# Holding back one batch's V load in a fused attention + MLP kernel: V of batch 3 behind the last x transpose of batch 2

## The chip, the cores and the metric

One core of a Trainium2 chip runs the whole program. The metric is device time in microseconds (us). The profile shows one execution with its own zero, so its span is some 2 us below the time. "Before" is the kernel as it was, "after" the changed one.

## The reference, cut to what matters

```python
# q, k, v: [8 batches, 8 heads, 576, 64]; w_in [512, 2048]; w_out [2048, 512]
scores = q @ k^T / 8 + alibi bias, masked to a causal window of 128
attn   = softmax(scores)
x      = (attn @ v) as [8*576 tokens, 512]
h      = x @ w_in
out    = (h * cos(h)) @ w_out
```

Tokens of all batches are one long row for the MLP, which runs in 9 chunks of 512 tokens. A batch has 576 tokens, so a chunk needs x of two batches: chunk 2 (tokens 1024 to 1535) begins in batch 1 and needs the first blocks of batch 2 almost at once.

## The kernel before

A planner in the kernel takes all operations with their dependences and estimated durations, orders them for each engine, and emits them with semaphores. It models the DMA engines too, so a changed dependence of a load can reorder TensorE's work far away from it. GpSimd issues all loads, in program order; the sync queue (SP) issues the transposes and the stores.

```python
def load_v(b, order=range(NBLK), after=()):
    for t in order:
        rows = 128 if t < 4 else 64
        op("pool", [lambda e, t=t, rows=rows: e.dma_start(
            vp[b % 2][0:rows, t, :, 0:64],
            v[b, :, 128 * t:128 * t + rows, :].rearrange("h p d -> p h d"))],
           r=[("vinit", b % 2)], w=[("v", b % 2, t)], dma=f"ldv{b % 2}{t}", ..., after=after)
...
def x_back(b, u, s, i):            # one head pair, 256 tokens of x: to xT (features x tokens)
    ...
    pr, G = u
    t0 = S * b + 256 * G
    if (b, pr + 4 * G) not in XPE:     # batches 0 and 1 do it on TensorE, the others by DMA
        o = op("sp", [lambda e: e.dma_start_transpose(
            xT[:, pr, t0:t0 + 256].rearrange("p (r t) -> p r t", r=2), xnat[i][:, :])],
            r=[("xnat", i)], w=xkeys(pr, t0, 256), dma=f"xb{i}", ...)
        xops.append(o)
        return
    ...
# main loop; moe1 is x @ w_in (L855 half chunks, L840 whole), moe2 is @ w_out (L866)
for c in range(NCH):
    ...                                # moe1 of chunk c
    second = moe2(c)
    if c + 1 < B:
        ...                            # attention of batch c + 1: scores, exp, mask, PV, x_back
    if c == 0:
        load_qk(2)
        load_v(2)
        load_qk(3)
        load_v(3)
    else:
        if 3 < c + 2 < B:
            load_v(c + 2, after=xops[3:4] if c > 2 else xops[-1:])
        if c + 3 < B:
            load_qk(c + 3, xops[-1:])
    ...                                # moe2 of chunk c, filled in around the attention
```

`xops` holds the nine x transposes of the batch in hand: head pairs 0 to 3 for the first 256 tokens, pairs 4 to 7 (the same heads, next 256 tokens), then the tail of 64 tokens. V has two buffers, so V of batch 3 goes where V of batch 1 was.

The softmax here doesn't subtract the row's maximum and nothing guards it: scores larger than these inputs give would overflow.

## Time and profile before

| | before |
|---|---|
| time, median of 3 | 313.44 us (313.19 to 313.70) |
| span of the profiled execution | 311.0 us |
| TensorE busy | 302.8 us, 97% |
| waits of TensorE for DMA after 21 us | one, 1.29 us, at the start of chunk 2 |
| first scores of batch 2 to those of batch 3 | 31.68 us |
| first scores of batch 3 to those of batch 4 | 30.34 us |

Three habits of reading serve here. First, ask TensorE's waits: on an engine that is full, the few gaps are all that a change outside it can win. Second, compare stages by a mark that recurs once a batch (the first scores, `L634 x12` in the chain of waits), and count the matmuls between the marks. Third, for a DMA read the time from issue to landing (its "flight" below), not the size: here it depends on what else is queued. A line of a timeline reads: start in us, length in us, engine, line of the kernel, operation, output<-inputs, shapes, count, and in brackets the idle time before it and what ended that. A line of a DMA queue gives packets, MB, and the time that its packets took as a share of the 16 engines' time, which can pass 100% where packets overlap. "Pair" is a head pair of x; "PV" is the product attn @ v. The prediction shows the lines of the kernel before.

### The profile page before, as it was taken

Reading aid. Unit: us, or ns where it says so; the run is one execution under the profiler, and the core shown is the slowest. Engines: PE = TensorE matmul, PEld = TensorE weight load, DVE = VectorE, ACT = ScalarE, POOL = GpSimd, SP = SyncE. Lnnn points to the kernel's source line nnn. Section 1 sums busy time; section 2 is a strip of 40 time slices with the busy share of each in tenths; the row PEclk is TensorE's granted clock in tenths of the full one; section 3 lists DMA queues with packets and bytes.
Section 4 is the critical chain, followed back from the end, with each engine's and each line's share of the span. In section 5 each row is a group of like instructions: output and inputs, shape, how many; then the busy total and the mean of one; then the engine's idle time right before and its main releaser. Section 6 shows DMA issues by size and latency. Waiting matters only on the chain.

```text
span 311.0 us, 6735 instructions
## 1 busy us (share of the span) xinstructions
PE 302.8 (97%) x2676; PEld 177.0 (57%) x2676; DVE 196.2 (63%) x443; ACT 205.8 (66%) x300; POOL 105.7 (34%) x134
## 2 busy tenths in 40 slices
PE   7799999999989999999999999999999999999996
PEld 4478546884578558845844454455445444444444
DVE  3898666786678748874885568767874881353000
ACT  7798946886478659765885478748874984462211
POOL 8999868620007300970555046405000000000000
PEclk9999999999999999999999999999999999999999
DMA  8999999999949992999999999999823100101112
GB/s 131 170 194 192 192 171 193 157 140 173 192 70 127 153 145 70 142 146 196 113 168 174 152 169 111 150 159 138 146 64 103 36 0 34 71 0 67 70 67 101
DMA packets 160894, 39.24 MB, mean 126 GB/s; under 512 B 148960, under 2 KB 156384, under 8 KB 160864
## 3 DMA queue, kind: packets, MB, share of 16 engines
q0 software_dynamic: 109552, 18.10, 78.7%
q1 hardware_dynamic: 51312, 20.72, 36.3%
q8 instruction: 21, 0.34, 0.5%
q14 instruction: 9, 0.07, 0.1%
HBM read 36.70 MB, written 9.44 MB: 148 GB/s over the span
## 4 chain that ended last, share of the span: by engine, by line
PE 91%; DMA 4%; DVE 2%; POOL 2%; issue 0%; ACT 0%; POOLq 0%
PE ps L866 39%; PE ps L855 20%; PE ps L840 20%; PE ps L634 4%; PE ps L728 3%; DMA knat<-in_k_dram 2%; DMA xT<-xnat 2%; PE ps L731 2%; PE ps L547 1%; PE ps L714 1%; PE ps L716 1%; DVE p L689 1%; PE ps L624 1%; POOL vp L464 1%; PE ps L803 1%; DVE emtail L528 0%
## 5 line engine op out<-in xcount | busy, mean ns | idle before, releaser
L866 PE MATMUL ps<-w_outb,gT 128*128 128x512 bf16 (+2 forms) x592 | 137.9, 374 | 0.0
L832 DVE TENSOR_TENSOR gT<-ps,cos 128x512 bf16<-128x512 f32 x144 | 94.9, 686 | 28.8 <-PE ps L866 15.0
L826 ACT ACTIVATE cos<-ps,halfpi 128x512 f32<-128x512 f32 x144 | 94.9, 685 | 22.4 <-PE ps L855 7.4
L866 PEld LDWEIGHTS ps<-w_outb,gT 128*128 128x128 bf16 x592 | 52.7, 98 | 53.3 <-issue 1.6
L671 ACT ACTIVATE p<-ps 128x768 bf16<-128x768 f32 (+1 forms) x64 | 54.7, 917 | 29.7 <-PE ps L634 15.2
L855 PE MATMUL ps<-xT,w_inb 128*128 128x256 bf16 x576 | 67.6, 273 | 1.3 <-DMA xT<-xnat 1.3
L840 PE MATMUL ps<-xT,w_inb 128*128 128x512 bf16 x288 | 64.8, 379 | 0.0
L855 PEld LDWEIGHTS ps<-xT,w_inb 128*128 128x128 bf16 x576 | 54.5, 98 | 8.7 <-DMA xT<-xnat 1.6
L464 POOL DMA_DIRECT2D vp<-in_v_dram x40 | 34.7, 894 | 64.3 <-DMA xT<-xnat 36.0
L840 PEld LDWEIGHTS ps<-xT,w_inb 128*128 128x128 bf16 x288 | 27.3, 98 | 32.2 <-DVE xtail L759 1.2
L420 ACT ACTIVATE ob<-ps 128x512 f32<-128x512 f32 (+2 forms) x25 | 14.5, 582 | 43.9 <-PE ps L866 43.7
L455 POOL DMA_DIRECT2D qnat<-in_q_dram x32 | 29.2, 914 | 41.4 <-DMA xT<-xtail 40.8
L455 POOL DMA_DIRECT2D knat<-in_k_dram x32 | 29.2, 913 | 1.7 <-issue 1.7
L689 DVE TENSOR_TENSOR p<-p,emask 128x1024 bf16<-128x1024 bf16 x32 | 21.8, 685 | 11.6 <-ACT p L671 11.4
L770 DVE TENSOR_TENSOR xnat<-ps,rec 128x256 bf16<-128x256 f32 x64 | 26.7, 421 | 2.0
L728 PEld LDWEIGHTS ps<-vp,p 128*128 128x128 bf16 x256 | 17.0, 97 | 14.2 <-issue 8.8
L728 PE MATMUL ps<-vp,p 128*128 128x65 bf16 x256 | 21.9, 193 | 0.4 <-DVE p L689 0.3
L731 PE MATMUL ps<-vp,p 128*128 128x65 bf16 x192 | 20.0, 193 | 0.0
L694 DVE TENSOR_TENSOR p<-p,emask 128x256 bf16<-128x256 bf16 x32 | 9.1, 283 | 17.2 <-ACT p L671 16.7
L492 ACT ACT_TABLE_LOAD x15 | 19.2, 1283 | 0.3
L634 PE MATMUL ps<-qt,kt 64*128 64x128 bf16 (+1 forms) x320 | 18.1, 238 | 0.5 <-DVE xT L421 0.3
L634 PEld LDWEIGHTS ps<-qt,kt 64*128 64x128 bf16 x320 | 11.8, 94 | 11.7 <-issue 7.8
(58 smaller groups left out, 168.3 us busy)
## 6 DMA issues: line engine op xcount, KB each, us to landing
out_dram<-ob SPq DMA_DIRECT2D x35, 256.0 KB, 3.3
vp<-in_v_dram POOLq DMA_DIRECT2D x32, 128.0 KB, 6.1
knat<-in_k_dram POOLq DMA_DIRECT2D x25, 128.0 KB, 9.1
qnat<-in_q_dram POOLq DMA_DIRECT2D x25, 128.0 KB, 9.1
w_inb<-in_moe_w_in_dram POOLq DMA_DIRECT2D x8, 256.0 KB, 8.4
w_outb<-in_moe_w_out_dram POOLq DMA_DIRECT2D x6, 256.0 KB, 14.4
qnat<-in_q_dram POOLq DMA_DIRECT2D x3, 256.0 KB, 10.1
knat<-in_k_dram POOLq DMA_DIRECT2D x3, 256.0 KB, 13.2
```

The lines of the kernel that those rows point to most:

```text
L455: op("pool", [lambda e: e.dma_start(nat[w][b % 2][0:rows, t, :].rearrange("p (h d) -> p h d", h=H), src[b, :, 128 * t:128 * t + rows, :].r ...
L464: op("pool", [lambda e, t=t, rows=rows: e.dma_start(vp[b % 2][0:rows, t, :, 0:64], v[b, :, 128 * t:128 * t + rows, :].rearrange("h p d -> ...
L634: ins = e.matmul(ps[:, banks[x], c0:c1], keys_ap(i, x, pr, kc), query_ap(i, x, pr, qb, nb), start=True, stop=True)
L671: op("act", lambda e: e.activation(P[i][:, :, lo:512], src_[:, :, lo:512], ACTF.Exp, scale=0.125), w=held + [("P", i)], occ=920 if u[1] el ...
L728: ins = e.matmul(o, P[i][:, x, d0:d0 + 128], V[:, kc, h, 0:65], start=True, stop=not two)
L731: ins = e.matmul(o, P[i][:, x, p0:p0 + 128], V[:, kc - 1, h, 0:65], start=False, stop=True)
L770: op("dve", lambda e: e.tensor_tensor(o, U[:, :, :, 0:64], rv[:, :, :, None].broadcast_to([128, 2, 2, 64]), ALU.mult), r=[("rec", ri)], w= ...
L826: op("act", lambda e: e.activation(cosb[ci][:, :], h, ACTF.Sin, bias=halfpi[:, 0:1]), r=["halfpi"], w=[("B", bank), ("cos", ci)], occ=586, ...
L832: op("dve", lambda e: e.tensor_tensor(o, h, cs, ALU.mult), r=[("cos", ci)], w=[("B", bank)] + keys, occ=606, lat=692, pri=3)
L840: op("pe", lambda e, kc=kc: e.matmul(ps[:, bank, :], w_in[:, kc, 128 * fc:128 * fc + 128], xT[:, kc, CH * c:CH * c + CH], start=(kc == 0), ...
L855: op("pe", lambda e, i=i, fc=fc, kc=kc: e.matmul(ps[:, bank, 256 * i:256 * i + 256], w_in[:, kc, 128 * fc:128 * fc + 128], xT[:, kc, t0:t0 ...
L866: op("pe", lambda e, fc=fc: e.matmul(ps[:, bank, 0:wd], gT[gi][:, fc, 128 * t:128 * t + 128], w_out[:, fc, c0:c0 + wd], start=(fc == 0), s ...
```

## The change

The intent is to get V of batch 3, needed only some 20 us after it lands (81.2 to 87.0 against 106.78), out of the way of the x transposes of batch 2.

```diff
                 load_qk(2)
                 load_v(2)
                 load_qk(3)
-                load_v(3)
             else:
-                if 3 < c + 2 < B:
-                    load_v(c + 2, after=xops[3:4] if c > 2 else xops[-1:])
+                if c + 2 < B:
+                    load_v(c + 2, after=xops[-1:] if c <= 2 else xops[3:4])
                 if c + 3 < B:
                     load_qk(c + 3, xops[-1:])
```

For c = 1 this loads V of batch 3 when the tail transpose of batch 2 has landed, ahead of q and k of batch 4. Other batches keep their rule.

## The prediction

> **What bounds the kernel now.** First the page, to see which engine is full and whether its clock is steady:
>
> ```profile
> PE 302.8 (97%) x2676; PEld 177.0 (57%) x2676; DVE 196.2 (63%) x443; ACT 205.8 (66%) x300; POOL 105.7 (34%) x134
> PEclk9999999999999999999999999999999999999999
> DMA  8999999999949992999999999999823100101112
> ```
>
> TensorE is the bound from end to end at an even clock, and the 16 DMA engines are full from the second slice to the 28th of 40 except around slices 12 and 16. So a change in DMA order is worth only what TensorE waits for DMA. The waits of TensorE from 21 us to the end, asked by themselves, have one single entry:
>
> ```profile
> PE ps L855 <- DMA xT<-xnat: 1.3, 1, 1.3
> ```
>
> (Weight loads also show waits of 0.1 to 0.5 us, but they run ahead of the matmuls and hold none of them up.) The timeline of TensorE places it, at the start of the first MoE product (L855 by half chunks, L840 by whole ones) of chunk 2, after the second MoE product (L866) of chunk 1 has filled in around the attention of batch 2 (scores L634, PV L728 and L731):
>
> ```profile
> 84.29 1.47 PE L866 MATMUL ps<-w_outb,gT 128*128 128x512 bf16 x6
> 85.59 0.49 PE L855 MATMUL ps<-xT,w_inb 128*128 128x256 bf16 x3
> 87.38 0.50 PE L855 MATMUL ps<-xT,w_inb 128*128 128x256 bf16 x3 [1.29 <-DMA xT<-xnat]
> ```
>
> A 128x256 product starts every 0.109 us (128 L855 in 13.98 us of chain time), so the fourth, which reads head pair 3 of x, should have started at 85.59 + 3 x 0.109 = 85.92. It started at 87.38: 1.46 us lost, of which 1.29 shows as idle because the ends of pipelined matmuls overlap.
>
> What held that x transpose? The timeline of the sync queue and of GpSimd:
>
> ```profile
> 76.00 3.87 SPq L791 DMA_TRANSPOSE xT<-xnat  x3
> 81.56 3.75 SPq L791 DMA_TRANSPOSE xT<-xnat  x3
> ```
> ```profile
> 57.42 0.92 POOL L464 DMA_DIRECT2D vp<-in_v_dram  x1
> 65.34 0.69 POOL L464 DMA_DIRECT2D vp<-in_v_dram  x1 [0.46 <-issue]
> 95.56 0.88 POOL L455 DMA_DIRECT2D qnat<-in_q_dram  x1 [29.53 <-DMA xT<-xtail]
> ```
>
> Head pairs 0 to 2 are issued from 76.00, pair 3 at 81.56; the chain of waits gives pair 3 as 5.77 us in flight, to 87.33. V of batch 3 (the L464 rows) is issued from 57.42 to 65.34. The view of that line for this window gives its time to landing:
>
> ```profile
> DMA to landing us min/median/max: 21.3/22.6/23.8
> ```
>
> So V of batch 3 sits behind a backlog and lands from 57.42 + 23.8 = 81.2 to 65.34 + 21.7 = 87.0 (the view of that block alone): exactly across the transposes that TensorE is about to need. Its own first reader, the PV product of batch 3, comes at 106.78. V is about 25 us early and in the way. The view of the DMA queues for 70 to 86 us:
>
> ```profile
> q0 software_dynamic: 11823, 1.49, 145.4%
> q1 hardware_dynamic: 2983, 1.38, 51.9%
> ```
>
> 11823 small packets in 16 us are 739 a microsecond; V of one batch is 8 heads x 576 rows = 4608 packets, 6.2 us of the shared engines.
>
> **What the Trainium skill says.** "DMA: Bandwidth & Descriptors", section "Queues, rings and completion order": each DMA engine alternates between the rows that have work, packet by packet, and a ring is consumed in order. The trace agrees: the x transposes of batch 2 issued at 76.0 to 78.6, with the software queue full, land in 6.6 to 7.5 us; those of batch 3 issued at 111.5 and 113.2, as that queue runs empty, land in 3.0 and 2.3 us. Same page, "Anatomy of one DMA": DMA engines do not wait on semaphores, the issuing sequencer does. The trace agrees: the 29.53 us in front of q of batch 4 is GpSimd waiting, while the engines work on. So a wait put before V also holds back everything GpSimd issues after it. Same page, "Specifications": below 512 B a transfer misses line rate. 148960 of the 160894 packets here are below, and the queues above moved 180 GB/s together, well under the 435 GB/s ceiling the page states; consistent, though no run here isolates packet size. "Perfetto Trace Analysis", section "Identifying the Most-Contended Engine", warns that matmul busy time is a bad measure of headroom; hence I use spacing of starts and waits, not the 97%.
>
> **The change part by part.** No work is added or removed: the same 5 V loads. GpSimd's order is unchanged (V of 3 already stood between q/k of 3 and q/k of 4); only a wait for the tail transpose of x of batch 2 moves from q of batch 4 to V of batch 3. So V is issued some 32 to 36 us later, and q/k of batch 4 come 5 loads later. This is what the kernel already does one batch later (V of 4 behind x of 3), so that stage of the old profile is my model.
>
> (1) Stage of batch 2. The last q/k load of batch 3 is issued at 56.75 and lands 22 to 24 us later, near 80. Without V the software queue is empty from there (old end: 87.0 less 6.2 = 80.8 by the packet count). Pair 3, still issued at 81.56, then lands as batch 3's did, 2.3 to 3.0 us later plus what is ahead of it: 84 to 85, before 85.92. TensorE's order up to this point is unchanged in the compiled program. Gain: the whole 1.46 us. Check from the chain, by the first scores of each batch:
>
> ```profile
> 72.21 0.60 PE ps L634 x12
> 103.89 0.62 PE ps L634 x12
> 134.23 0.62 PE ps L634 x12
> ```
>
> 31.68 us for the stalled stage against 30.34 for the next, with 53 L866 and 128 L855 in each by the chain: a difference of 1.34, close to the 1.46.
>
> (2) V of batch 3 in time? In the old stage of batch 3 V of batch 4 starts at 125.07, when the tail transpose (issued at 122.36) has landed, 18.3 us after that batch's first PV product. For batch 2 that gives 74.64 + 18.3 = 92.9. V then issues over 4.2 us and lands 5.6 to 8.1 us after issue (as V of 4 does), so its first two blocks are there near 99 to 101. The first PV product of batch 3 is at 106.78 - 1.46 = 105.3. Slack 4 us or more: cost 0.
>
> (3) q/k of batch 4. Issued from 97 to 106 instead of 95.6 to 104, landing up to 13 us later (as those of batch 5 did), 119; their transposes stand behind batch 3's x, about 122. Cost 0.
>
> (4) x transposes of batch 3 now fly beside 4608 more packets. The same load, V and q/k, 3 x 4608 = 13824 packets, took from about 128.0 to 147.6 in the old batch 4 (counted in the trace's packet records; the queue view of 128 to 148 us shows 14063 of that queue's), ending 10.3 us after the first PV at 137.3. Moved to batch 3 it ends near 115.5. The transposes of pairs 0 to 3, now issued at 106.8, 108.0, 110.0 and 111.7, will take about 6.5 us (old batch 4: 6.4 to 6.6), pair 3 some 6.0 as the queue runs empty, so land at 113.3, 114.5, 116.5 and 117.7. TensorE wants the first at 117.31 - 1.46 = 115.8 and pair 2 at 116.0: a wait of up to 0.5. Without help pair 3 would cost 117.7 - 116.1 = 1.6, giving everything back. But the kernel's planner knows of the traffic and has reordered here: 3 L855, 2 L866, a PV group, 3 L855, an L866, a PV group, an L866, and only then pair 3. That is some 0.33 + 0.43 + 0.25 + 0.33 + 0.22 + 0.25 + 0.22 = 2.0 us later than the first, 117.8: no wait. Cost 0 to 0.5, say 0.3.
>
> (5) Later stages get another mix of the same matmuls; chunk 4 begins with tokens of batch 3 only, so it does not depend on batch 4's transposes. Cost 0 with a scatter of 0.3.
>
> Sum: 313.44 - 1.46 + 0.3 = 312.3 us.
>
> **The rivals.** A: the stall moves whole to batch 3, whose transposes now share the engines; 313.4, no change. For it: landings of 6.5 us whenever the software queue is full. Against: the reorder buys 2.0 us. B: V of batch 3 becomes a new wait on PV, or q/k of 4 arrive late and delay scores of batch 4; 314 to 317. Against: the old kernel does this for batches 4 to 7 and shows no such wait. C: the old stage's wait does not go, because the transposes queue behind each other and behind the stores on the sync queue; 313.3. Against: batch 3's landings of 2.3 to 3.0 us. D: a larger gain, because the other engines also run smoother; 311.5 at best, since TensorE has no other wait after 21 us.
>
> **Range and chances.** The gain is capped by the 1.46 us plus scatter, and A and C end at about 313.4. So 312.3, with 311.5 to 313.5 eight times in ten. 2% is 6.3 us; faster by that is impossible on what TensorE waits for (0.01), slower by it would need B at its worst (0.02); within 2%: 0.97.
>
> **What would show it.** Right: the wait of L855 on the x transpose at 85.9 is gone, pair 3 lands within 4 us, V is issued near 93 and lands within 8 us, first scores of batch 3 near 102.4. Step (4) is told by the L855 group at 115.8: no wait or one of 0.5 at most. Wrong: an entry of PV waiting on the V load, of scores on q/k transposes, or a wait of over 1 us there.

## The result, and the profile after

| | before | after |
|---|---|---|
| time, medians of 6 runs each, same rounds | 313.73 us (313.19 to 314.38) | 313.82 us (313.61 to 314.75) |
| ratio after / before, 95% interval | | 1.0006 (0.9989 to 1.0023) |
| first scores, batch 2 to 3 | 31.68 us | 30.30 us |
| first scores, batch 3 to 4, as read | 30.34 us | 33.10 us |
| the same, with equal numbers of L866 | 30.34 us | 31.80 us |

The times are the same; the interval excludes the gain of 1.1 us (0.9964) that was predicted, so this was not merely hidden by scatter.

TensorE's waits from 21 us on, of the changed kernel:

```profile
PE ps L855 <- DMA xT<-xnat: 1.4, 1, 1.4
PE ps L866 <- issue: 0.6, 4, 0.2
PE ps L855 <- DMA w_inb<-in_moe_w_in_dram: 0.2, 1, 0.2
```

Again one wait for an x transpose, and of the same size. (The 0.6 us of "issue" falls where this trace misses 37 of the 2676 matmul records: 2639 on its page. The 0.2 us for weights is at 28.4 us, before the two kernels differ.) But it is elsewhere. TensorE's timeline at the start of chunk 2, after:

```profile
86.41 0.82 PE L855 MATMUL ps<-xT,w_inb 128*128 128x256 bf16 x6
```

All six run through: the old wait is gone. At the start of chunk 3, whose x is batch 3's, the kernel before had no wait:

```profile
117.31 0.82 PE L855 MATMUL ps<-xT,w_inb 128*128 128x256 bf16 x6
```

The changed kernel has one:

```profile
116.75 0.38 PE L855 MATMUL ps<-xT,w_inb 128*128 128x256 bf16 x2
118.51 0.28 PE L855 MATMUL ps<-xT,w_inb 128*128 128x256 bf16 x1 [1.38 <-DMA xT<-xnat]
118.84 0.38 PE L866 MATMUL ps<-w_outb,gT 128*128 128x512 bf16 x1
```

The third product, which reads head pair 2, should have started at 116.75 + 2 x 0.109 = 116.97 and started at 118.51: 1.54 us. The sync queue and GpSimd, after:

```profile
82.38 3.75 SPq L791 DMA_TRANSPOSE xT<-xnat  x3
...
110.34 0.52 SPq L880 DMA_DIRECT2D out_dram<-ob  x1
110.91 4.24 SPq L791 DMA_TRANSPOSE xT<-xnat  x3
```
```profile
94.86 4.21 POOL L464 DMA_DIRECT2D vp<-in_v_dram  x5 [35.95 <-DMA xT<-xtail]
```

V of batch 3 now starts at 94.86, as one batch of five loads. Time to landing of the transpose issued at 82.38 (pair 3 of batch 2) and of the one issued at 110.91 (pair 2 of batch 3), two answers of the view of that line:

```profile
DMA to landing us min/median/max: 2.4/2.4/2.4
```
```profile
DMA to landing us min/median/max: 7.6/7.6/7.6
```

The first took 5.8 us before, the second 3.0 (issued at 111.5 there). The queues in 104 to 120 us, first of the kernel before, then of the changed one:

```profile
q0 software_dynamic: 5467, 0.69, 70.9%
```
```profile
q0 software_dynamic: 9931, 1.25, 125.3%
```

The software queue (GpSimd's loads) has 4464 packets more there, nearly the 4608 of one V. They are not V's own: V landed from 100.36 to 106.67, and the first x transpose of batch 3 was issued at 107.70. They are q and k of batch 4, which V, standing ahead of them, has pushed back: these ten loads landed from 107.07 to 118.80, and from 100.67 to 113.15 before. The chain of waits after, for the stages:

```profile
73.03 0.60 PE ps L634 x12
103.33 0.62 PE ps L634 x12
136.43 0.60 PE ps L634 x12
```

The stage of batch 2 gives 31.68 - 30.30 = 1.38 us. The stage of batch 3 reads 33.10, but the planner put 59 L866 between these marks where it had put 53 (counted in the complete trace of the run with the load early and the order of the change, below; the trace of the changed kernel itself shows 55, as records are missing). 6 x 0.216 = 1.30 us of that is work moved, leaving 31.80, which is 1.46 us longer than before. Gain and loss cancel. The first mark is also 0.82 us later than before (73.03 against 72.21). Most of that was there before the kernels differ: the first PV product of batch 1 is at 40.33 against 39.61, and the load that was moved stood at 57.42. Across the profiles that mark lies between 72.2 and 73.0 us, and at 74.75 in one that began at a reduced clock: the start of the kernel scatters by an amount comparable to the effect. Stages are therefore the better witness, and times need many rounds.

### The profile page after: what moved, and what is told of

Its sections match the earlier page's. It is cut to its first block, busy times and chain, and to the rows that moved or that the text cites. A ratio compares the mean times of both kernels' runs of the same rounds, so it can differ in the third digit from the quotient of the medians.

```text
span 312.1 us, 6701 instructions
## 1 busy us (share of the span) xinstructions
PE 301.8 (97%) x2639; PEld 177.5 (57%) x2676; DVE 196.8 (63%) x444; ACT 205.5 (66%) x299; POOL 105.8 (34%) x134
## 4 chain that ended last, share of the span: by engine, by line
PE 83%; DMA 8%; POOL 7%; issue 1%; ACT 0%; DVE 0%; POOLq 0%
PE ps L866 37%; PE ps L840 20%; PE ps L855 16%; DMA vp<-in_v_dram 5%; PE ps L634 4%; DMA xT<-xnat 2%; PE ps L728 2%; POOL w_inb L471 2%; PE ps L731 2%; POOL vp L464 1%; POOL w_outb L478 1%; PE ps L714 1%; POOL qnat L428 1%; POOL knat L428 1%; PE ps L716 1%
## 5 line engine op out<-in xcount | busy, mean ns | idle before, releaser
L866 PE MATMUL ps<-w_outb,gT 128*128 128x512 bf16 (+2 forms) x565 | 133.3, 373 | 1.7 <-issue 0.6
L866 PEld LDWEIGHTS ps<-w_outb,gT 128*128 128x128 bf16 x592 | 52.7, 98 | 52.7 <-issue 1.6
L840 PE MATMUL ps<-xT,w_inb 128*128 128x512 bf16 x279 | 64.0, 379 | 0.5
```

What stands on the lines that cost most here:

```text
L840: op("pe", lambda e, kc=kc: e.matmul(ps[:, bank, :], w_in[:, kc, 128 * fc:128 * fc + 128], xT[:, kc, CH * c:CH * c + CH], start=(kc == 0), ...
L866: op("pe", lambda e, fc=fc: e.matmul(ps[:, bank, 0:wd], gT[gi][:, fc, 128 * t:128 * t + 128], w_out[:, fc, c0:c0 + wd], start=(fc == 0), s ...
```

## The experiments

Theory 1: x transposes are late when the software queue has packets beside them; the move of V took some 4600 packets from beside batch 2's and put as many (q and k of batch 4, pushed back) beside batch 3's, and the wait moved with them. Theory 2: the load's move did its good, and the replanned order of the engines lost it again. Theory 3: such a wait of TensorE is worth nothing at the end, since a later stage takes the time up.

The edits are shown in part: comments are added, and the lines that pick up `v3` (the first of V's five loads), `held` (the tail transpose) and `p2`, `p3` are left out.

### The load late, the order of before

```diff
         R.schedule()
+        R.all[v3].preds[held] = DATA      # V of 3 waits for the tail transpose of batch 2
+        late = R.all[v3:v3 + NBLK]         # emitted after it; every engine's own order is unchanged
+        R.order = [o for o in R.order if o not in late]
+        at = R.order.index(held) + 1
+        R.order[at:at] = late
```

> The kernel before with its instruction order on TensorE, VectorE, ScalarE and the sync queue untouched, but V of batch 3 held back on GpSimd until the tail transpose of batch 2 has landed, as in the change. Theory 1 (traffic: the wait moves to batch 3 because its x transposes now share the engines with V and q/k): the wait of batch 2 is gone, in batch 3 pairs 2 and 3 land some 7.6 and 6.3 us after issue, and since the old order asks for pair 3 right after pair 2 the wait there is about 1.9 us; time 0.3 to 0.6 us above before. Theory 2 (the replanned order of the change lost the time, not the traffic): no wait over 0.5 us in batch 3 and a time 1.4 us below before.

Measured: 313.19 us against 313.26 for before (ratio 1.0002, 0.9985 to 1.0020). First scores 72.40, 102.70, 134.25: stages of 30.30 and 31.55 us. TensorE in batch 3:

```profile
116.12 0.38 PE L855 MATMUL ps<-xT,w_inb 128*128 128x256 bf16 x2
117.52 0.72 PE L855 MATMUL ps<-xT,w_inb 128*128 128x256 bf16 x4 [1.01 <-DMA xT<-xnat]
```

With the old order the same thing happens: 1.38 us won, 1.21 lost. So theory 2 is not needed. The size was not as I expected: 1.0 us of idle instead of 1.9. Both pairs flew shorter than in the changed kernel: pair 2 for 7.20 us (110.27 to 117.47), pair 3, issued at 112.05, for 5.64 (to 117.69). Pair 3 landed only 0.22 us after pair 2, so most of its lateness hides behind the wait for pair 2. Alone it would have cost more than a microsecond in this order, for it was wanted at 116.12 + 3 x 0.109 = 116.45.

### The load early, the order of the change

```diff
         R.schedule()
+        del R.all[v3].preds[held]
+        for o in R.all[v3:v3 + NBLK]:
+            o.preds.pop(held, None)        # V of 3 waits for its buffer alone
```

> The changed kernel with its replanned instruction order on all engines untouched, but V of batch 3 no longer held: it loads early as before, and the wait for the tail transpose stands before q of batch 4 again. Theory 1 (traffic): the wait of 1.3 to 1.5 us is back in batch 2's stage, and there is none in batch 3's; time within 0.3 us of before. Theory 2 (the replanned order itself costs): a wait or a longer stage of 1.4 us remains in batch 3's stage as well, time about 1.4 us above before.

Measured: 313.35 us against 313.26 (1.0003, 0.9988 to 1.0018). The one wait is back in batch 2's stage:

```profile
87.58 0.50 PE L855 MATMUL ps<-xT,w_inb 128*128 128x256 bf16 x3 [1.16 <-DMA xT<-xnat]
```

Stages of 31.55 (72.54 to 104.09) and 31.64 us (to 135.73), the second again with 59 L866, so 30.34. The replanned order by itself costs nothing and the wait follows the load: theory 1 holds, theory 2 falls. These two runs, before and after form a square: load early or late, order old or new. Only the load decides where TensorE waits, and none of the four differs from before in time.

### No V of batch 3 at all

```diff
         R.schedule()
+        for o in R.all[v3:v3 + NBLK]:
+            o.fn = []                      # no transfer; batch 3 reads V of batch 1 (wrong on purpose)
```

> The kernel before with V of batch 3 not loaded at all (batch 3 reads V of batch 1, so the output is wrong on purpose); every other instruction is in its old place. This takes the disputed traffic away from both stages. Theory 1: no wait in either stage, time 1.4 to 1.5 us below before. Theory 3 (the wait of TensorE is worth nothing at the end, as the next stage would take the time up again): time within 0.3 us of before.

Measured: 312.02 us against 313.26, ratio 0.9963 (0.9947 to 0.9979), output wrong as intended. TensorE has no DMA wait after 21 us. First scores, from its chain of waits:

```profile
72.38 0.60 PE ps L634 x12
102.68 0.62 PE ps L634 x12
133.02 0.62 PE ps L634 x12
```

Stages of 30.30 and 30.34 us: the good one of each kernel. Theory 3 falls: the wait is worth 1.2 us at the end. With V's 4608 packets gone from beside batch 2's transposes, and none pushed back to beside batch 3's, neither stage waits. What was predicted as the gain was there to be had. (What the square and this run do not try: leaving V where the change put it, and holding q and k of batch 4 back until pair 3 of batch 3 has landed.)

### V behind pair 3 instead of the last, twice

If V may stand beside neither set, it could fly in the hole of the DMA engines between 86 and 94 us.

```diff
-                    load_v(c + 2, after=xops[-1:] if c <= 2 else xops[3:4])
+                    load_v(c + 2, after=xops[3:4] if c != 2 else xops[-1:])
```

> The change with one word of it altered: V of batch 3 waits for the x transpose of head pair 3 of batch 2, the last one that the next MoE chunk reads first, instead of the last of the nine; q and k of batch 4 still wait for the last. Theory 1: V is issued near 85 and flies in the hole where the engines have little to do (86 to 94 us), so it is beside neither the pairs 0 to 3 of batch 2 nor those of batch 3: no wait in either, time 1.2 to 1.5 us below before. Against it: V slows the remaining x transposes of batch 2 and with them the start of q/k of batch 4 by 1 to 2 us, so that half of the wait in batch 3 stays: 0.7 us below before.

Measured: 313.03 us against 313.26 (1.0004, 0.9980 to 1.0029). The profiled execution began late at a reduced clock, and its six times ran from 312.43 to 314.73, so it was run once more.

> The kernel with V of batch 3 behind pair 3 of batch 2 once more, for its time only: its first profile fell in an execution whose start was 2.4 us late at a reduced TensorE clock in the first slices, and two of six times lay above 314. By its stages (30.77 and 30.33 us between first scores against 31.68 and 30.34 before) it should be 0.9 us below before; if the stages do not carry through to the end, it is within 0.3 us of before.

Measured: 313.25 us against 313.29 (0.9996, 0.9972 to 1.0020): no gain, a miss. TensorE's timeline of the second run:

```profile
96.05 6.94 PE L855 MATMUL ps<-xT,w_inb 128*128 128x256 bf16 x62 [1.83 <-DMA xT<-xnat]
```

The wait moved to a third place, the second half of chunk 2, which needs pairs 4 to 7 of batch 2: V was issued from 84.97, and the transpose issued at 87.84 took 8.2 us. In the first run this wait was 0.30 us. (TensorE's order is that of the kernel before here; on the sync queue one store and one k transpose of batch 3 have changed places.) The hole in the DMA engines was no free place: it is the time of the next transposes. The two stages together take 62.65 us in the second run and 61.10 in the first, against 62.02 before, so the size of such a wait changes from one execution to the next.

### A store taken out from ahead of the transposes, in the changed kernel, twice

In batch 3 a store of 256 KB was issued at 110.34, between pairs 1 and 2. My prediction had counted V, q and k beside pair 2, and did not name this store. (The stage that it took its flights from had one in the same place, though: a store at 140.34, pair 2 of the old batch 4 at 140.87, and that pair took 6.62 us.)

```diff
         R.schedule()
+        sp = [o for o in R.order if o.eng[0] == "sp"]
+        st = sp[sp.index(p2) - 1]          # p2, p3: x transposes of pairs 2 and 3 of batch 3
+        R.order.remove(st)
+        R.order.insert(R.order.index(p3) + 1, st)
```

> The changed kernel with one store of 256 KB moved on the sync queue: in the stage of batch 3 it stood between pairs 1 and 2 of the x transposes, now it comes after pair 3; all else is in its place. Theory 1a (pair 2 is late because the store and the software queue share the engines with it, and the store also takes its turn on the sync queue before it): pair 2 is issued about 0.5 us earlier and flies some 6.5 us or less instead of 7.6, so the wait of 1.4 us before L855 in batch 3 shrinks to 0.3 or less, and time falls by about 1.1 us against the changed kernel. Theory 1b (the software queue with V and q/k alone sets the flight): the pair still takes over 7 us and the wait stays above 0.8 us.

Measured: 312.63 us against 313.29 (0.9978, 0.9955 to 1.0002). Pair 2 was issued at 109.6, took 6.7 us and landed at 116.3, just when it was wanted; there was no DMA wait in either stage. By the lines drawn beforehand that speaks for theory 1a.

> The changed kernel with the store after pair 3 of batch 3 once more, for its time: the first runs gave a ratio of 0.9978 with an interval that just touches 1. No DMA wait of TensorE in the stages of batches 2 and 3, and 0.5 to 1.2 us below before.

Measured: 312.93 us against 313.18 (0.9995, 0.9976 to 1.0013), and in this execution the wait was there:

```profile
117.59 0.28 PE L855 MATMUL ps<-xT,w_inb 128*128 128x256 bf16 x1 [0.87 <-DMA xT<-xnat]
```

Pair 2 was issued at 110.5 here, since pair 0 ahead of it held the sync queue for 1.87 us instead of 1.17 and the start was 0.3 us later, and took 7.0 us. By the same lines this execution speaks for theory 1b (a flight over 7 us, a wait above 0.8), and my expectation missed. With the store in its old place the late load with the old order had 7.20 us and 1.01 us, hardly more. So whether the store is a part of the delay here is not shown, and no gain in time is established, for both intervals include 1.

### The same with a store in the kernel before

```diff
         R.schedule()
+        sp = [o for o in R.order if o.eng[0] == "sp"]
+        st = sp[sp.index(p3) - 1]          # now batch 2's; the store that stood just ahead of pair 3
+        R.order.remove(st)
+        R.order.insert(R.order.index(p3) + 1, st)
```

> The kernel before, V of batch 3 early, with the same treatment of a store in the stage of batch 2: the store of 256 KB that stood just ahead of pair 3 comes just after it, all else in its place. If the store's share of the engines was part of that wait as it was in batch 3 of the changed kernel, pair 3 (which is itself ready only near 81.5, so it cannot be issued much earlier) lands 0.8 to 1.0 us earlier, the wait of 1.3 us falls to 0.3 to 0.6, and time is 0.7 to 1.0 us below before. If V's packets alone hold pair 3 until they are through, it still lands near 87 and the wait stays above 1.0.

Measured: 312.26 us against 313.18, ratio 0.9975 (0.9958 to 0.9991). The wait fell from 1.29 to 0.46 us:

```profile
86.31 0.94 PE L855 MATMUL ps<-xT,w_inb 128*128 128x256 bf16 x5 [0.46 <-DMA xT<-xnat]
```

It is now for pair 1, which took 9.04 us to land (77.23 to 86.27), while pair 3 took 5.15 from 81.55. Pairs 2 and 3 then landed at 86.49 and 86.70, each just ahead of its product, so that pair 3's product is still 0.8 us later than without any wait. The gain in time is as expected; by the stage it is 0.61 us (31.07 against 31.68), and pair 3 landed 0.63 us earlier where 0.8 to 1.0 was expected. Here, unlike in batch 3, the store's place does change the time.

### One pair of batch 2 transposed by TensorE, V early as before

```diff
-XPE = [(b, u) for b in range(2) for u in range(8)] 
+XPE = [(b, u) for b in range(2) for u in range(8)] + [(2, 3)]
```

> The kernel before, V of batch 3 early as ever, with one of the eight full x transposes of batch 2, head pair 3, done by TensorE (two 128x128 transposes and a copy from PSUM) instead of the DMA queue. TensorE's order is otherwise unchanged. Theory 1: what was waited for no longer flies beside V, so the wait of 1.3 us goes at a cost of about 0.2 us of TensorE: time 1.1 to 1.3 us below before, no new wait in batch 3. Against it: pair 2, issued at 78.6 and landed at 85.2 before, is next in line and needed at 85.8; if it is later here, a wait of up to 0.5 us stays.

Measured: 311.97 us against 313.29, ratio 0.9956 (0.9935 to 0.9977). No DMA wait after 21 us; first scores at 72.99, 103.36 and 133.70, stages of 30.37 and 30.34 us. TensorE:

```profile
82.58 0.28 PE L803 MATMUL ps<-ident,xnat 128*128 128x128 bf16 x2
...
86.45 0.82 PE L855 MATMUL ps<-xT,w_inb 128*128 128x256 bf16 x6
```

Two matmuls of 128 columns, which delay the next L866 by about 0.1 us (82.58 to 82.70), replace a DMA transpose that was late. All the gain predicted for the change is had here, with V where it was. Its six times lie between 311.85 and 312.28, those of before in the same rounds (eleven) between 312.36 and 314.59. This is the version to keep: it beats the kernel before, and the changed kernel, which it did not meet in the same rounds, is no faster than that. The wait is gone in its one profile; pairs 0 to 2 still fly beside V there (6.35 to 7.38 us).

## Why the prediction was right or wrong

The prediction (312.3, range 311.5 to 313.5) was wrong: 313.82 was measured and there is no gain. Its steps:

1. **Stage of batch 2: right.** The wait at 85.9 went, pair 3 landed in 2.4 us (predicted within 4), and the stage gave 1.38 us where 1.46 were predicted.
2. **V in time: right.** It was issued at 94.86, with the start 0.82 us late against a predicted 92.9, and landed 5.5 to 8.7 us later (predicted within 8); no PV product waited for it.
3. **q and k of batch 4 in time: right.** No scores waited.
4. **x transposes of batch 3: the step that failed.** It said "a wait of up to 0.5" for pair 2 and booked 0.3 us; the measured wait was 1.38 us of idle, 1.54 by starts, over the 1 us that the prediction had named as a sign of being wrong. The mechanism, transposes slowed by the software queue's traffic, was right; the term that was mis-sized is the flight of pair 2. The time from its issue to its need was read rightly: 6.0 us (110.0 to 116.0), measured 6.06 (110.91 to 116.97). Its flight was taken as 6.5 us from the old batch 4 and was 7.55. Then the defence: the replanned order was counted on to hide 2.0 us, and it nearly did for pair 3, which landed at 119.00, 1.92 us after the old order would have asked for it (116.75 + 3 x 0.109 = 117.08). It cost nothing here; had pair 2 been in time, the new order would have asked for it at 118.75 (2.0 us after the first product, as in the store run without a wait), 0.25 us too early. But that order defers only pair 3; pair 2 is asked for 0.22 us after the first product in either order.
   Why pair 2 flew 1.05 us longer than in the old batch 4 is left open. The profile before held such flights already, 7.50 us (issued at 77.25) and 7.61 (at 168.64), so the 6.4 to 6.6 us of one stage were too narrow a model. The store between pairs 1 and 2 cannot be the whole answer, since the old batch 4 had one too. The working also misread that model in one place, which did not enter the 6.5 us: the first PV product of the old batch 4 is at 136.52, not 137.3, and the queue's load had 14064 packets, the last of which started at 148.46 (counted in the trace's packet records). Moved to batch 3 the queue then ends near 117.2, not 115.5; measured, its last packet started at 118.46, with the start 0.82 us late, just as pair 2 landed (118.47).
5. **Later stages: right so far as seen.** Neither kernel shows a DMA wait after chunk 3, and the run with the load early and the new order agrees with before within its interval.

Rival A of the prediction, "the stall moves whole to batch 3", is what happened. It was named with the right reason for it (long landings when the software queue is full) and set aside for a defence that did not cover the critical item. That the transposes land late beside this traffic is shown; that the engines alternate between the two queues packet by packet, which the prediction says the trace agrees with, no run here isolates.

## What to carry to other kernels

Moving a load only helps if there is a place where its packets, and those of the loads that it pushes back, fly beside nothing urgent; before betting on it, list which transfers are in flight at the new place, and check for each the moment it is needed, not only for the one that was late before. Read landing times as a function of the queue's load, and allow for their scatter: a transfer that is needed within a microsecond of its usual landing is late in some executions. Where bulk loads cannot be kept away from a small urgent transfer, take that one off the DMA engines if a compute path costs less, as two short matmuls did here.

## What the Trainium skill lacked or had wrong

- "DMA: Bandwidth & Descriptors", section "Queues, rings and completion order", tells that a DMA engine alternates between rows packet by packet, but not what this costs a small transfer: the transpose of one head pair (128 x 256 bf16, 64 KB) landed 2.3 to 4.4 us after issue when no packet of the software queue moved meanwhile (2.3 in most cases), and up to 9.0 us beside that queue.
- The same page, section "Anatomy of one DMA", fits a GpSimd-issued DMA as 2.0 us + bytes / 436e3. For a V block of 128 KB that is 2.3 us by our estimate from the fit; with 128-byte packets and q/k transposes beside it the first one landed after 5.5 us, and the five loads queued behind other loads after 21.3 to 23.8 us. The shortest landing of any such block of q, k or V in these profiles is 3.45 us. The fit has no term for packet size (the page speaks of small descriptors elsewhere) or for what is queued ahead; how the difference divides between the two, no run here shows.
- No page that I used says by how much landing times vary between executions of one program: the transposes of one kernel were late by 0.30 us in one execution (the one that began at a reduced clock) and by 1.83 us in another.
